# Reordering the opening of an attention kernel: key loads, pooled sums and value sums moved between queues, engines and units

## The chip, the cores and the metric

The kernel runs on one core of one Trainium2 chip. The metric is the device time of one execution in microseconds, taken as the median of several executions. The core has a matrix engine (TensorE, PE in the profile), a vector engine (VectorE, DVE), a scalar engine (ScalarE, ACT), a general engine (GpSimd, POOL) and an engine that mostly starts transfers (SyncE, SP). ACT and POOL start transfers too; each of the three has a queue of its own.

## The reference, cut to what matters

The program computes an attention layer and then two mixture-of-experts layers on its output. The change touches the attention alone:

```python
B, H, S, D = 4, 8, 576, 64          # batches, heads, positions, head size
q_d, k_d, v_d = means over groups of 4 positions of q, k, v     # 144 rows each
out_up   = repeat(softmax(q_d @ k_d.T * scale) @ v_d, 4)        # pooled attention
out_local = softmax(q @ k.T * scale where |i - j| < 4) @ v      # local attention
x = out_up + out_local              # 2304 tokens of 512, input of the experts
```

## The kernel before, in words

The attention is a list of 38 units, numbered here from 0 in the order in which they are pushed. Eighteen are local units, one for each tile of 128 tokens (`Local(t)`); twenty are pooled units, five for each batch (`Pooled(b, u)`). The order is written out by hand: local tiles 0 to 3 are units 0 to 3; batch 0's pooled units are 4, 5, 6, 8 and 9, with tile 4 as unit 7; tile 5 is unit 10, batch 1's pooled units begin at 11, tile 6 is unit 14.

`push(unit)` writes one unit's scores and soft step, the transposes (`turn`) of the unit two before it, the work that was scheduled for this unit (`later`, filled by `schedule(n, f)`, which puts f n units ahead), and the values step (`values`) of the unit three before it. PE, ACT, DVE and POOL carry out their instructions in just this written order. SP's order is set by a planner that sorts transfers by the time at which it believes them ready.

The pooled units need sums over four positions. `pool_qk(b, n)` makes those of queries (`qd`) and keys (`kd`): for batch 0 all on DVE, one reduction for each of twelve 128x576 pieces (the second halves of the keys, `kd[:, i, 1]`, at L776); for batch 1 all on GpSimd, where `pooled_on_gpsimd` makes one 128x576x4 piece in three adds (L759, L789). `pool_v(b, n)` makes the sums of the values (`vd`) on PE with a matrix of ones (`fours`, L798 and L805), which ACT copies out (L800, L809); when it has read batch b's values it starts the load of those of batch b+1, since there is one buffer (`NVG = 1`).

Loads: `load_qk(b)` brings a batch's queries (for batch 1 on GpSimd's queue, else on SP's) and its keys in two halves (SP and ACT). `load_local(t)` brings the value windows of a tile, a half each on SP and ACT. `load_wall` brings the routing weights on GpSimd's queue, copied by DVE `WALLP` units later. Batch 1's key buffer is zeroed by GpSimd first (`zero_keys`), because half of each block must stay zero. `start_1`, `start_2` and `start_3` are done with units 0, 1 and 2: zeroed buffers, distances and masks for the local units, constants for the routing.

Of the kernel before, what the change touches and what calls it, by code (L numbers as in the profile page):

```python
# [15 lines left out]
OP = mybir.AluOpType  # L16
AX = mybir.AxisListType
# [60 lines left out]
D2 = 3  # L78
NEP = 3
EPS = 48  # L80
ONDVE = (0,)
ONPOOLQ, ONPOOLQD, QDP, WALLP = (1,), (2,), 0, 12
NVG = 1
XB = 8
UB = 4
LOADQK = (-1, -1, 5, 9)
POOLQK = (2, 4, 6, 10)
POOLV = (3, 4, 6, 10)
QKS = 4
VS = 0  # L90
PATTERN = ((4, 0, 1), (2, 3))
POOLED = (3, 5, 9, 12)

# [10 lines left out]
def moe_attention_kernel(ctx, tc, q, k, v, w_skip, w_gate, w1, w2, g2, n2, noise, u1, u2, out, dbg=None):  # L104
# [507 lines left out]
    with ExitStack() as actx:  # L612
# [20 lines left out]
        def load_v(b, e=nc.sync):  # L633
            t = ld.tile([128, 4, DM], F32, name="v0", bufs=NVG)
            u = ld.tile([64, DM], F32, name="v1", bufs=NVG)
            r0 = b * S * DM
            e.dma_start(t, v[r0:r0 + 512 * DM].rearrange("(p c d) -> p c d", p=128, d=DM))
            e.dma_start(u, v[r0 + 512 * DM:r0 + S * DM].rearrange("(p d) -> p d", d=DM))
            return t, u
# [12 lines left out]
        def zero_keys(i, e):  # L652
            t = shared.tile([128, 2, 4, S], F32, name=f"kT{i}", bufs=1, tag=f"shared{i}")
            kTs.append(t)
            fill(e, t[:, 0])
            fill(e, t[:, 1])
# [16 lines left out]
        def zero_pooled_exps(e):  # L673

            t = at.tile([128, 2, NPOOL + 16], F32, name=f"ep{len(eps)}", bufs=1)
            e.memset(t[:, :, NPOOL:], 0.0)
            e.memset(t[:, :, NPOOL:NPOOL + 1], 1.0)
            eps.append(t)

        def pooled_ones(e):  # L680


            t = at.tile([128, 2, H, D + 1], F32, name=f"vd{len(vds)}", bufs=1)
            h = H // 2
            e.memset(t[:, 1], 0.0)
            e.memset(t[0:32, 1, :, D:D + 1], 4e-9)
            e.memset(t[0:16, 1, h:, D:D + 1], 0.0)
            e.memset(t[:, 0, :, D:D + 1], 4.0)
            e.memset(t[0:16, 1, 0:h, D:D + 1], 4.0)
            e.memset(t[32:48, 1, h:, D:D + 1], 4.0)  # L690
            vds.append(t)
# [24 lines left out]
        def start_1():  # L716
            for n in range(3, NES):
                zero_exps(P)
            for n in range(3, NVW):
                zero_values(P)  # L720
            zero_keys(1, P)
            pooled_ones(P)
            zero_pooled_exps(P)
            zero_pooled_exps(P)
            for d in offsets:
                distances(d)

        def start_2():
            for n in range(2, NEP):
                zero_pooled_exps(P)  # L730
            pooled_ones(P)
            nc.gpsimd.dma_start(x_d[0:1], kTs[1][0:1, 1, 0, 0:DM + 16])
            for n in range(1, NVG):
                vgs[n] = load_v(n)
            for t in range(2, NVW):
                load_local(t)
            load_qk(1)

        def start_3():
            routing_constants()  # L740
            for d in offsets:
                mask(d)


        fours = at.tile([128, 32], F32, name="fours", bufs=1)
# [2 lines left out]
        def load_qk(b):  # L748

            held["k", b % 2] = b  # L750
            qT[b] = at.tile([128, 4, S], F32, name="qT", bufs=2)
            (nc.gpsimd if b == 1 else nc.sync).dma_start(qT[b], q[b])
            for g in range(2):
                (nc.sync, nc.scalar)[g].dma_start(kTs[b % 2][g:128:2, g], k[b, 64 * g:64 * g + 64])

        def pooled_on_gpsimd(o, x):
            x = x.rearrange("p a (g r) -> p a g r", r=4)
            for j in range(1, 4):
                nc.gpsimd.tensor_tensor(o, x[:, :, :, 0] if j == 1 else o, x[:, :, :, j], op=OP.add)  # L759
# [5 lines left out]
        def pool_qk(b, n):  # L765


            assert held["k", b % 2] == b
            held["kd", b % 2] = (b, n)
            if n == 0 and b not in ONPOOLQD:  # L770
                qd[b] = at.tile([128, 4, NPOOL], F32, name="qd", bufs=2)
            kd, kT = kds[b % 2], kTs[b % 2]
            if n >= 8 and b in ONDVE:
                for i in range(n - 8, 4, 3):
                    o, x = kd[:, i, 1], kT[:, 1, i]
                    nc.vector.tensor_reduce(o, x.rearrange("p (g r) -> p g r", r=4), axis=AX.X, op=OP.add)  # L776
            elif b in ONPOOLQ and n < 8:
                if n == 0:
                    pooled_on_gpsimd(kd[:, :, 0], kT[:, 0])
                    pooled_on_gpsimd(qd[b], qT[b])  # L780
            elif n % 2 == 0 and n < 8 and b in ONPOOLQD:
                pass
            elif n < 8:
                i = n // 2
                o, x = (qd[b][:, i], qT[b][:, i]) if n % 2 == 0 else (kd[:, i, 0], kT[:, 0, i])
                nc.vector.tensor_reduce(o, x.rearrange("p (g r) -> p g r", r=4), axis=AX.X, op=OP.add)
            else:
                o, x = kd[:, :, 1], kT[:, 1].rearrange("p a (g r) -> p a g r", r=4)
                nc.gpsimd.tensor_tensor(o, x[:, :, :, 0] if n == 8 else o, x[:, :, :, n - 7], op=OP.add)  # L789
# [95 lines left out]
        def load_local(t):  # L885

            vw = vws[t % NVW]
            for g in range(2):
                o = N * DM + (2 * t + g) * WV * 1024
                (nc.sync, nc.scalar)[g].dma_start(vw[g:2 * WV:2, g],  # L890
                                  v[o:o + WV * 1024].rearrange("(p s c) -> p s c", s=4, c=256))
# [153 lines left out]
        def schedule(n, f, *args):  # L1045
            later.setdefault(len(pipe) + n, []).append(lambda: f(*args))
# [142 lines left out]
        for t in range(NT):  # L1189
            for b in range(B):  # L1190
                if LOADQK[b] == t:
                    load_qk(b)
                    if b in ONPOOLQD:
                        schedule(QDP, pool_q, b)
                if POOLQK[b] == t:
                    for n in range(8):
                        schedule(n // QKS, pool_qk, b, n)
                    for n in range(3):
                        schedule(n // 2 if b in ONDVE else n, pool_qk, b, n + 8)
                if b == 0 and t == EXP4 and UPE:  # L1200
                    schedule(0, expansion)
                if POOLV[b] == t:
                    schedule(0, pool_v, b, 0)
                    schedule(VS, pool_v, b, 1)
            if t == 3:
                load_wall()
            if t < 3:
                schedule(0, lambda: None)
                schedule(0, lambda: None)
                schedule(0, (start_1, start_2, start_3)[t])  # L1210
            push(Local(t))
            for b, u in pooled_after.get(t, []):
                push(Pooled(b, u))
# [757 lines left out]
```

## Time and profile before

| what | us |
|---|---|
| median of 3 runs (lowest, highest) | 777.15 (775.94, 778.45) |
| the profiled execution | 780.45 |
| its span, first to last instruction | 778.5 |
| outside of the span | 1.95 |
| PE busy in the span | 755.6 (97%) |

The trace is of the one profiled execution, whose time is 3.30 us above the median; differences worked out in it are taken off the median. Times in the rows count from the start of the span. A busy PE counts modelled ends of pipelined matmuls.

### The profile page before, as it was taken

What the parts mean: (1) busy time and instruction counts of PE and PEld (TensorE: products, weight loads), DVE (VectorE), ACT (ScalarE), POOL (GpSimd) and SP (SyncE); (2) the same over time, 40 slices, a digit from 0 to 9 for tenths busy, and PEclk for the clock granted to TensorE, in tenths of its full rate; (3) what the DMA queues carried; (4) which work ended last, traced back from release to release, by engine and by line L of the source; (5) the groups of instructions that cost most, each with busy time, mean ns of one, the idle gap of its engine ahead of it and who ended that gap; (6) DMA issues with size and microseconds to landing.
All of it is one profiled execution on the core that took longest, in us unless ns stands there. A gap on an engine that the chain in (4) does not pass through costs nothing.

```text
span 778.5 us, 15158 instructions
## 1 busy us (share of the span) xinstructions
PE 755.6 (97%) x6215; PEld 664.3 (85%) x6215; DVE 351.3 (45%) x805; ACT 249.6 (32%) x492; POOL 255.0 (33%) x257
## 2 busy tenths in 40 slices
PE   6999998999999999999999999999999999999996
PEld 3567785999999999989998998998998997997984
DVE  8776877510111755469854343262242343342200
ACT  3444553111112133224334343233233242333211
POOL 8782422211232351133364205215115115002012
PEclk9899999999999999999999999999999999999998
DMA  8988578699988872331556626526436336333013
GB/s 287 301 263 272 156 187 283 183 371 355 314 313 259 307 282 97 103 69 43 144 170 172 180 82 166 112 87 174 105 106 159 80 110 159 87 84 67 8 16 46
DMA packets 61128, 131.51 MB, mean 169 GB/s; under 512 B 15585, under 2 KB 16928, under 8 KB 59520
## 3 DMA queue, kind: packets, MB, share of 16 engines
q1 hardware_dynamic: 31552, 56.64, 23.4%
q10 hardware_dynamic: 17248, 46.66, 16.6%
q0 software_dynamic: 12256, 27.21, 16.6%
q8 instruction: 50, 0.82, 0.4%
q14 instruction: 22, 0.18, 0.1%
HBM read 101.86 MB, written 23.91 MB: 162 GB/s over the span
## 4 chain that ended last, share of the span: by engine, by line
PE 76%; issue 2%; DVE 1%; DMA 1%; POOL 0%; ACT 0%; POOLq 0%; DVEq 0%; ACTq 0%
PE pY L1612 27%; PE pH L1595 26%; PE pH L560 9%; PE pY L573 9%; PE pT L1580 2%; PE pT L592 1%; PE pT L539 1%; DMA rows<-x_d,ix2g 1%; PE pT L346 1%; PE pH L581 0%; POOL out L317 0%; DVE w L337 0%; PE pH L597 0%; PE pT L223 0%; DVE hl L1600 0%
## 5 line engine op out<-in xcount | busy, mean ns | idle before, releaser
L1612 PE MATMUL pY<-w,hh 128*128 128x512 f32 (+6 forms) x640 | 201.5, 396 | 0.0
L1595 PE MATMUL pH<-xh,w 128*128 128x256 f32 (+7 forms) x1024 | 196.0, 303 | 0.0
L1595 PEld LDWEIGHTS pH<-xh,w 128*128 128x128 f32 x1024 | 162.9, 188 | 0.8
L1612 PEld LDWEIGHTS pY<-w,hh 128*128 128x128 f32 (+6 forms) x640 | 115.0, 183 | 27.6
L1271 DVE TENSOR_TENSOR w<-stg,w 128x1024 fp32r<-128x1024 f32 x64 | 82.5, 1298 | 108.1 <-ACT w L1270 108.0
L1612 PE MATMUL pY<-w,hl 128*128 128x512 f32 (+6 forms) x320 | 125.6, 393 | 0.0
L1595 PE MATMUL pH<-xl,w 128*128 128x256 f32 (+7 forms) x512 | 123.5, 302 | 0.0
L1600 DVE SCALAR_TENSOR_TENSOR hl<-pH,hh 128x256 fp32r<-128x256 f32 (+7 forms) x128 | 57.0, 474 | 128.8 <-ACT hh L1599 128.5
L317 POOL DMA_INDIRECT out<-yo,ix2w x35 | 68.8, 1967 | 130.0 <-ACT yo L1614 121.5
L1599 ACT ACTIVATE hh<-pH 128x256 fp32r<-128x256 f32 (+7 forms) x128 | 49.3, 424 | 151.8 <-PE pH L1595 151.6
L1595 PEld LDWEIGHTS pH<-xl,w 128*128 128x128 f32 x512 | 90.1, 188 | 0.0
L312 POOL DMA_INDIRECT rows<-x_d,ix2g x32 | 36.2, 1132 | 155.4 <-PE pT L1580 144.2
L1612 PEld LDWEIGHTS pY<-w,hl 128*128 128x128 f32 (+6 forms) x320 | 58.5, 183 | 15.3
L573 PE MATMUL pY<-hT,w 128*128 128x112 f32 (+7 forms) x512 | 69.2, 296 | 0.0
L1270 ACT ACTIVATE w<-stg 128x1024 fp32r<-128x1024 f32 x64 | 66.8, 1054 | 6.8 <-DMA stg<-in_moe_w 6.8
L1614 ACT ACTIVATE yo<-pY,gt 128x512 f32<-128x512 f32 (+6 forms) x35 | 24.1, 688 | 138.3 <-PE pY L1612 77.4
L573 PEld LDWEIGHTS pY<-hT,w 128*128 128x128 f32 x512 | 67.4, 190 | 0.2
L560 PE MATMUL pH<-xT,w 128*128 128x200 f32 (+6 forms) x448 | 66.2, 301 | 0.0
L560 PEld LDWEIGHTS pH<-xT,w 128*128 128x128 f32 x448 | 61.1, 190 | 1.8 <-issue 1.7
L317 POOL DMA_INDIRECT l_d<-x,ix1w x15 | 14.3, 953 | 87.9 <-DVE x L600 87.0
L575 DVE COPY yT<-pY 128x224 f32<-128x224 f32 (+7 forms) x16 | 7.5, 471 | 73.8 <-PE pY L573 73.8
L1006 POOL TENSOR_TENSOR x<-x,up 128x512 f32<-128x512 f32 x15 | 19.3, 1291 | 42.5 <-DMA up<-od 32.6
(426 smaller groups left out, 851.4 us busy)
## 6 DMA issues: line engine op xcount, KB each, us to landing
w<-in_moe_w ACTq DMA_DIRECT2D x16, 2048.0 KB, 12.5
stg<-in_moe_w SPq DMA_DIRECT2D x64, 512.0 KB, 3.6
x_d<-x SPq DMA_DIRECT2D x18, 264.0 KB, 4.1
out<-zero ACTq DMA_DIRECT2D x3, 1536.0 KB, 7.6
up<-od SPq DMA_DIRECT2D x14, 256.0 KB, 5.1
qT<-in_q SPq DMA_DIRECT2D x3, 1152.0 KB, 5.5
vw<-in_v SPq DMA_DIRECT2D x18, 192.0 KB, 5.5
vw<-in_v ACTq DMA_DIRECT2D x18, 192.0 KB, 5.5
```

The source lines that it names most:

```text
L312: return nc.gpsimd.indirect_dma_start(out=dst, out_offset=None, in_=x_d[0:n + 1], in_offset=bass.IndirectOffsetOnAxis(ap=idx, axis=0))
L317: return nc.gpsimd.indirect_dma_start(out=dst, out_offset=bass.IndirectOffsetOnAxis(ap=idx, axis=0), in_=src, in_offset=None, **kw)
L560: nc.tensor.matmul(self.p[:, j], w[:, k, f * 128:(f + 1) * 128], self.xT[:, k], start=k == 0, stop=k == KD - 1)
L573: nc.tensor.matmul(p[:, j], w[:, f, d * 128:(d + 1) * 128], self.hT[:, f], start=f == 0, stop=f == KF - 1)
L1006: e.tensor_tensor(xs[t][:, 0:DM], xs[t][:, 0:DM], ups[t], op=OP.add)
L1270: nc.scalar.activation(hi[:, c], st[i], AF.Copy)
L1271: V.tensor_tensor(lo[:, c], st[i], hi[:, c].bitcast(F32), op=OP.subtract)
L1595: nc.tensor.matmul(p, w[:, k, fs], self.x[ch][n][:, k, 0:ch[1] - ch[0]], start=k == 0 and i == 0, stop=k == KD - 1 and i == 2)
L1599: nc.scalar.activation(hi, p, AF.Relu)
L1600: V.scalar_tensor_tensor(lo, p, 0.0, hi.bitcast(F32), op0=OP.max, op1=OP.subtract)
L1612: nc.tensor.matmul(p, h[:, f], w[:, f], start=f == 0 and i == 0, stop=f == KF - 1 and i == 2)
L1614: nc.scalar.activation(o, p, AF.Copy, scale=gate[0:n])
```

## The change

It alters where and when the attention's opening work is issued; every sum and load is still made once. Batch 0's values are summed with unit 6 (was 3) and batch 1's with unit 11 (was 7), batch 2's with unit 15 (was 14). Batch 0's second-half key sums go from DVE (four reductions) to GpSimd (three adds). Batch 1's queries are loaded on GpSimd's queue right after the key buffer is zeroed, and both halves of its keys on SP's queue. Routing constants (to unit 10), masks (to unit 6), distances and the last zeroed buffers (to unit 3) come later, and so do the routing weights' load (before unit 10) and copy (unit 16).

```diff
-ONDVE = (0,)
-ONPOOLQ, ONPOOLQD, QDP, WALLP = (1,), (2,), 0, 12
+ATONCE = (0,)
+ONPOOLQ, ONPOOLQD, QDP, WALLT, WALLP = (1,), (2,), 0, 5, 6
-POOLV = (3, 4, 6, 10)
+POOLV = (3, 5, 6, 10)
-VS = 0
+VD = (3, 1, 1, 0)
@@ start_1
             zero_keys(1, P)
+            load_qk(1)
             pooled_ones(P)
             zero_pooled_exps(P)
             zero_pooled_exps(P)
+
+        def start_2():
+            for t in range(2, NVW):
+                load_local(t)
+            load_k(1)
+
+        def start_3():
+            schedule(0, start_4)
+            schedule(3, lambda: [mask(d) for d in offsets])
+            schedule(7, routing_constants)
+
+        def start_4():
+            for n in range(2, NEP):
+                zero_pooled_exps(P)
             for d in offsets:
                 distances(d)
-
-        def start_2():
-            for n in range(2, NEP):
-                zero_pooled_exps(P)
             pooled_ones(P)
             nc.gpsimd.dma_start(x_d[0:1], kTs[1][0:1, 1, 0, 0:DM + 16])
-            for n in range(1, NVG):
-                vgs[n] = load_v(n)
-            for t in range(2, NVW):
-                load_local(t)
-            load_qk(1)
-
-        def start_3():
-            routing_constants()
-            for d in offsets:
-                mask(d)
@@ load_qk
             (nc.gpsimd if b == 1 else nc.sync).dma_start(qT[b], q[b])
+            if b != 1:
+                load_k(b)
+
+        def load_k(b):
             for g in range(2):
-                (nc.sync, nc.scalar)[g].dma_start(kTs[b % 2][g:128:2, g], k[b, 64 * g:64 * g + 64])
+                (nc.sync, nc.sync if b == 1 else nc.scalar)[g].dma_start(kTs[b % 2][g:128:2, g], k[b, 64 * g:64 * g + 64])
@@ pool_qk
-            if n >= 8 and b in ONDVE:
-                for i in range(n - 8, 4, 3):
-                    o, x = kd[:, i, 1], kT[:, 1, i]
-                    nc.vector.tensor_reduce(o, x.rearrange("p (g r) -> p g r", r=4), axis=AX.X, op=OP.add)
+            if n >= 8 and b in ATONCE:
+                if n == 8:
+                    pooled_on_gpsimd(kd[:, :, 1], kT[:, 1])
@@ the loop over tiles
-                        schedule(n // 2 if b in ONDVE else n, pool_qk, b, n + 8)
+                        schedule(n // 2 if b in ATONCE else n, pool_qk, b, n + 8)
-                    schedule(0, pool_v, b, 0)
-                    schedule(VS, pool_v, b, 1)
-            if t == 3:
+                    schedule(VD[b], pool_v, b, 0)
+                    schedule(VD[b], pool_v, b, 1)
+            if t == WALLT:
                 load_wall()
```

## Rows read from the trace of the kernel before

**Rows 1.** The page's head and its line of the matrix engine.

```profile
span 778.5 us, 15158 instructions
...
PE 755.6 (97%) x6215; PEld 664.3 (85%) x6215; DVE 351.3 (45%) x805; ACT 249.6 (32%) x492; POOL 255.0 (33%) x257
```

**Rows 2.** Windows: span, busy time (instructions) by engine, PE clock, DMA share.

```profile
core 0: us, PE busy (x) PEld busy (x) DVE busy (x) ACT busy (x) POOL busy (x), PEclk, DMA share, GB/s
0.00:10.00 10.00, 7.90 (x53) 3.22 (x53) 7.03 (x15) 5.30 (x4) 8.79 (x24) 1.00 0.81 289
10.00:20.00 10.00, 5.50 (x124) 3.07 (x117) 9.11 (x20) 1.60 (x4) 8.96 (x37) 0.84 1.01 285
20.00:30.00 10.00, 9.38 (x123) 5.69 (x120) 8.51 (x18) 4.30 (x10) 5.82 (x34) 0.65 1.00 333
...
60.00:70.00 10.00, 10.00 (x164) 7.62 (x156) 6.71 (x20) 5.12 (x16) 1.28 (x1) 1.00 0.84 265
70.00:80.00 10.00, 8.84 (x162) 5.84 (x160) 6.71 (x16) 4.35 (x13) 2.50 (x2) 1.00 0.87 282
```

**Rows 3.** Windows of the two stretches of lower clock.

```profile
16.80:27.00 10.20, 7.59 (x72) 3.62 (x76) 9.30 (x20) 3.70 (x9) 7.24 (x46) 0.50 1.00 342
...
44.10:47.50 3.40, 3.40 (x17) 3.01 (x15) 1.92 (x6) 1.22 (x3) 3.24 (x3) 0.50 0.99 334
```

**Rows 4.** Waits of PE from 14 to 50 us: total, times, longest.

```profile
PE pT L798 <- DMA v<-in_v: 4.7, 2, 4.5
PE pA L832 <- POOL kd L789: 1.8, 1, 1.8
```

**Rows 5.** Timeline of PE: start, length, line, output and input, idle before.

```profile
13.63 0.66 PE L982 MATMUL pT<-ident,e 128*128 128x128 f32 x4
18.79 1.93 PE L798 MATMUL pT<-v,fours 128*32 128x512 f32 x8 [4.50 <-DMA v<-in_v]
...
24.02 1.19 PE L832 MATMUL pA<-kd,qd 128*32 128x288 f32 x8
...
31.73 0.30 PE L951 MATMUL pA<-mask,identb 128*128 128x304 bf16 x1
...
33.35 1.07 PE L798 MATMUL pT<-v,fours 128*32 128x512 f32 x8 [0.18 <-DMA v<-in_v]
34.42 0.61 PE L805 MATMUL pT<-v,fours 64*16 64x256 f32 x4
...
42.97 0.69 PE L832 MATMUL pA<-kd,qd 128*32 128x288 f32 x8 [1.85 <-POOL kd L789]
...
51.19 1.06 PE L798 MATMUL pT<-v,fours 128*32 128x512 f32 x8
```

**Rows 6.** Timeline of POOL, 13 to 43 us.

```profile
13.02 0.52 POOL L685 MEMSET vd<- 128x520 f32 x1
...
14.59 1.65 POOL L702 IOTA dj<- 32x38 f32 x8
...
17.52 0.72 POOL L732 DMA_DIRECT2D x_d<-kT  x1
18.24 0.63 POOL L752 DMA_DIRECT2D qT<-in_q  x1
...
28.38 1.29 POOL L759 TENSOR_TENSOR kd<-kT 128x576 f32<-128x576 f32 x1 [3.94 <-DMA kT<-in_k]
29.74 3.51 POOL L759 TENSOR_TENSOR kd<-kd,kT 128x576 f32<-128x576 f32 x2
...
39.42 3.49 POOL L789 TENSOR_TENSOR kd<-kd,kT 128x576 f32<-128x576 f32 x2
```

**Rows 7.** Timeline of DVE: batch 0's second-half key sums.

```profile
15.99 2.06 DVE L776 TENSOR_REDUCE kd<-kT 128x144 f32<-128x576 f32 x3
```

**Rows 8.** Timeline of ACT's queue: the second half of batch 1's keys.

```profile
18.82 0.52 ACTq L754 DMA_DIRECT2D kT<-in_k  x1
```

**Rows 9.** DMA issues at 18.7, 20, 52.5 and 62.5 us: KB, time to landing.

```profile
kT<-in_k ACTq DMA_DIRECT2D x1, 576.0 KB, 9.4
...
v<-in_v SPq DMA_DIRECT2D x1, 1024.0 KB, 12.4
...
v<-in_v SPq DMA_DIRECT2D x1, 1024.0 KB, 9.2
...
qT<-in_q SPq DMA_DIRECT2D x1, 1152.0 KB, 5.5
```

## The prediction

> **What bounds the kernel now.** I read the page first, then the windows in steps of 10 us, then PE's waits, and then the opening engine by engine. The page says that PE is busy for 97% of the span [rows 1]: the kernel can only get shorter where PE stands still, works at the lower clock, or does work that it need not do. The windows show where that is: PE works 5.50 of the 10 us from 10 to 20, at a mean clock of 0.84, and from 20 to 30 its clock is 0.65 [rows 2]. From 60 to 70 it works without a hole [rows 2], so a unit that starts earlier there ends earlier. PE's waits from 14 to 50 us are nearly two events [rows 4]: 4.5 us for batch 0's values at 18.79, and 1.85 us for a key sum of GpSimd at 42.97 [rows 5]. A low clock follows each: PE runs at the lower of its two levels (0.50, that is 1.2 of 2.4 GHz) from 16.8 to 27.0 and from 44.1 to 47.5 [rows 3], and eight equal matmuls take 1.93 us at 18.79, but 1.07 at 33.35 [rows 5].
>
> The second wait closes a chain that starts in the DMA queues. The second half of batch 1's keys is issued on ACT's queue at 18.82 [rows 8] and lands 9.4 us later [rows 9], at 28.2. GpSimd, idle for 3.94 us by then, starts batch 1's sums at 28.38 and ends them at 39.42 + 3.49 = 42.91 [rows 6]; unit 11's scores start at 42.97 [rows 5]. That chain, 28.4 + 14.5 + 0.1, sets the time of unit 11, and all later PE work hangs on it. What the change is worth is read there.
>
> **Part 1: batch 0's key sums and value sums.** Before, PE reads the values' sums in front of unit 0's values step and waits for them. With the sums at unit 6, it goes on after its transposes at 13.63 + 0.66 = 14.3 [rows 5] with unit 0's values (its window must have landed, as ACT's copy must; both were asked for by then), and then meets unit 4's scores, which need the batch's key sums. On GpSimd these now stand behind the key buffer's zeroing (ends at 13.0), the issue of batch 1's queries (0.63 and a gap, 0.7) and 1.57 us of small fills (13.02 to 14.59); the three adds cost what the same three cost for batch 1, 28.38 to 29.74 + 3.46, that is 4.82 us [rows 6]. Sum: 13.0 + 0.7 + 1.6 + 4.8 = 20.1. DVE's eight other reductions are shorter than that once four of 0.66 to 0.74 us (three in 2.06 [rows 7]) are gone. So unit 4's scores start at 20.1, where they stood at 24.02 [rows 5].
>
> The row says that four reductions of DVE (2.7 us) become 4.8 us of GpSimd. The Trainium skill, GPSIMD Engine Reference, section Engine selection, speaks against that: it puts reductions along the free dimension on VectorE and calls GpSimd about half as fast for adds of two inputs. Left on DVE, by that rule, the sums would come behind DVE's other reductions, some 2.7 us after about 19.7, so 22.4; the engine's lower rate would then matter only if GpSimd were the later one. No run here shows it yet.
>
> **Part 2: batch 1's loads.** The queries' issue moves from 18.24 [rows 6] to 13.1, the keys' second half from 18.82 [rows 8] to 13.1, as soon as its buffer is zeroed; both halves now queue on SP behind the first windows, and ACT is not held by that issue. How early do they land? Not earlier than 13.1 + 9.4 = 22.5, not later than the 28.2 of before. Asked for by 13.7 are queries and keys of two batches, one batch of values and four windows, by their sizes 7.47 MB in all; the first 20 us move 2.89 + 2.85, and the rest of 1.73 MB takes 5.2 us at 333 GB/s [rows 2], so everything has landed by 25.2. The keys stand in front of the queries in this line, so I take 24.3. GpSimd is then free: after the adds at 20.1 it has distances (1.7), fills (1.2) and the zero row's transfer (0.7) to do, spans 14.59 to 18.24 of before [rows 6], which ends at 23.75. Batch 1's sums take 14.5, as before: unit 11 may start at 24.3 + 14.5 + 0.1 = 38.9, instead of 42.97.
>
> Does PE get there by then? From unit 4 to unit 7 it took 31.73 - 24.02 = 7.7 us, from there to its wait 41.1 - 31.7 = 9.4 [rows 5]. It gains batch 0's value sums (1.07 + 0.61 = 1.7) and loses batch 1's (1.7, and 0.2 of waiting). If the low clock lasts to 27.0 as before, 3.9 us more of this work lies in it than before and cost 2 us more: 20.1 + 7.7 + 1.7 + 2.0 = 31.5, then 9.4 - 1.9, so 39.0. If the higher level is back a third sooner, 37.2. I take 39.0 for unit 11: both chains meet there. That is 4.0 us earlier than before.
>
> **Part 3: what then follows unit 11.** Batch 1's value sums stood in the shadow of that wait; now they come behind it: 1.6 us of PE at the high level [rows 5] that nothing covers. For the low stretch behind unit 11 (3.4 us at half rate, 1.7 us lost [rows 3]) I take the value of before, as PE may still wait up to 1.8 us; the other end is that it is gone. Routing constants (18.9 to 22.2 before, 3.3 us) and the weights' transfers (2.2 us) stood in front of GpSimd's wait for the keys, and now stand behind batch 1's sums: GpSimd gets to its first residual add some 0.9 us later than the 52.65 of before, while PE needs it at about 57.7 - 2.4; this stays covered, and if it were not it would cost what is missing of the 1.7 us left. Masks, distances and wall copy lie beside other work on DVE, cover for about 2 us of them being PE's own queue.
>
> Sum: -4.0 + 1.6 = -2.4 us on a profiled 780.45, so 778.05 for an execution like that one, and 777.15 - 2.4 = **774.7** as the median, as that execution lies 3.3 us above it.
>
> **Rivals.**
> *No low stretch behind unit 11.* If PE arrives no earlier than the sums, as the sum above has it, PE never rests before 11 and the 1.7 us stay: 774.7 - 1.7 = 773.0. For it speaks that the only two low stretches of the opening follow holes of PE [rows 3, 5]; against it, that PE's arrival has 2 us of uncertainty.
>
> *The keys land no earlier.* The engines are at shares of 1.01 and 1.00 from 10 to 30 us [rows 2]; an earlier issue then only divides the same bandwidth. Unit 11 stays at 42.8, the value sums are added: -0.2 + 1.6 = 778.5. Against it: 1.73 MB remain at 20 us, not more. The Trainium skill, DMA: Bandwidth & Descriptors, section Issuing engines are not separate DMA queues, says just this of moving a transfer to another engine's queue: it saves the issue time alone. By that rule the move from ACT to SP gives nothing, and only the earlier time of issue can; the shares in the trace agree with a full set of engines.
>
> *The third batch's values come late* (the other side). Their one buffer is free only when batch 1's sums have read it, now behind unit 11: 39.0 + 1.0 for scores and transposes + 1.0, issue at 41.0, 42.0 in a low stretch, instead of 34.5. PE asks for them at unit 15, in the place of 51.19 [rows 5]: 51.19 - 2.4 + 1.2 for the pooled unit now in front = 50.0. The load has 8 us. Loads of this kind took 9.2 and 12.4 us with other megabytes in the queue, a load of 1152 KB with little in front took 5.5 [rows 9]; since batch 2's queries and keys have by then had the queue for themselves, I take 7.5, no stall. At 12.4 PE waits 4.4 and falls to the low level once more: 774.7 + 4.4 + 1.7 = 780.8. It is slower than the bound from 11.1 us of landing on.
>
> *Given back later.* From 60 to 80 us the DMA share is 0.84 and 0.87, and PE has a hole of 1.2 us from 70 to 80 [rows 2]. If loads there set the pace, units 11 to 20 come earlier and wait there: 777.1.
>
> **How the numbers follow.** A difference of 0.3% (2.3 us; 774.8 and 779.5) is about what a measurement of this kernel can tell from none. Chances: forecast 0.36 (its own range 773.6 to 775.8, a little over half of it under 774.8); no low stretch 0.20, faster; keys no earlier 0.16, same but for 0.04 slower; third values late 0.16, of this 0.13 slower; given back 0.12, same. Faster 0.20 + 0.20 = 0.40, same 0.16 + 0.12 + 0.03 + 0.12 = 0.43, slower 0.04 + 0.13 = 0.17. The time is 774.7; the range reaches from 772.3, under the second case with keys at 23.8, to 779.5, which leaves out most of the late values.
>
> **What will show it.** Right: no wait for values before unit 0's values step; unit 4's scores at about 20; batch 1's sums on GpSimd from 24 to 39; unit 11 at 39 with value sums right behind it; from there to 120 us the same rows, some 2.4 us earlier. Wrong: keys landing at 27 or later, GpSimd not free when they land, PE waiting for batch 2's values at unit 15, or SP holding a transfer behind the two key halves so that windows come late.

## The result: 0.64% slower, and the profile after

Over twelve executions each the changed kernel takes 785.49 us (782.42 to 788.68) and the one before 780.62 us (775.94 to 784.0): ratio 1.0064, interval 1.0042 to 1.0086. Forecast was 774.7, with 779.5 as the upper end. Of the 10.8 us between forecast and time 3.5 lie in the base: 777.15 was the median of three executions of the kernel before, 780.62 is that of twelve. The profiled execution of after took 785.6 us, its span 783.6, which is 5.1 us longer than that of before [rows 1].

The page's head and its line of PE, after:

```profile
span 783.6 us, 15153 instructions
...
PE 756.6 (97%) x6212; PEld 667.1 (85%) x6215; DVE 356.6 (46%) x801; ACT 251.0 (32%) x492; POOL 257.8 (33%) x260
```

PE is busy 1.0 us longer than before, in that longer span: the rest is PE standing still. The timeline of PE after (columns as in [rows 5]; lines are 4 higher than before: scores are L833 and L836, value sums L802 and L809):

```profile
20.26 1.24 PE L836 MATMUL pA<-kd,qd 128*32 128x288 f32 x6 [1.95 <-POOL ep L676]
22.15 0.67 PE L836 MATMUL pA<-kd,qd 128*32 128x288 f32 x2 [0.65 <-DVE kd L790]
...
27.49 1.07 PE L802 MATMUL pT<-v,fours 128*32 128x512 f32 x8
...
30.94 0.29 PE L955 MATMUL pA<-mask,identb 128*128 128x304 bf16 x1 [0.83 <-DVE mask L710]
...
36.10 1.30 PE L870 MATMUL pB<-vd,epT 128*128 128x130 f32 x6 [2.14 <-DVE x L1004]
...
42.31 0.67 PE L836 MATMUL pA<-kd,qd 128*32 128x288 f32 x8
...
43.39 1.06 PE L802 MATMUL pT<-v,fours 128*32 128x512 f32 x8
...
80.25 0.71 PE L1016 MATMUL pT<-ident,x 128*128 128x128 f32 x4 [2.85 <-POOL x L1010]
```

Unit 4 starts at 20.26, unit 7 at 30.94, near the forecast (20.1 and 31.5); the releaser printed at 20.26, `POOL ep`, is the small fill that follows GpSimd's key sums, which end at 20.21. Unit 7 is there by another sum than the forecast's, though: 2.0 us had been counted for a low clock up to 27.0, and in this profile the clock is 1.00 from 13 to 36; the waits of 0.65 us for VectorE's key sums and 0.83 for a mask stand in its place. From unit 7 to unit 11 PE takes 11.4 us where 7.5 were forecast, and unit 11 is at 42.31, not 39.0. GpSimd is not the reason here; its timeline (idle before in brackets) shows batch 0's second-half sums, batch 1's, and the residual add of tile 4:

```profile
15.34 1.28 POOL L764 TENSOR_TENSOR kd<-kT 128x576 f32<-128x576 f32 x1
16.70 3.51 POOL L764 TENSOR_TENSOR kd<-kd,kT 128x576 f32<-128x576 f32 x2
...
24.67 1.25 POOL L764 TENSOR_TENSOR kd<-kT 128x576 f32<-128x576 f32 x1 [1.01 <-DMA kT<-in_k]
...
29.46 1.25 POOL L764 TENSOR_TENSOR qd<-qT 128x576 f32<-128x576 f32 x1
30.79 3.49 POOL L764 TENSOR_TENSOR qd<-qd,qT 128x576 f32<-128x576 f32 x2
...
35.59 3.45 POOL L793 TENSOR_TENSOR kd<-kd,kT 128x576 f32<-128x576 f32 x2
...
78.94 1.26 POOL L1010 TENSOR_TENSOR x<-x,up 128x512 f32<-128x512 f32 x1 [14.94 <-DMA up<-od]
```

The keys' first sum starts at 24.67 and the sums are done at 39.04: both as forecast (24.3, 38.9). What PE waits for is VectorE, whose timeline has the four mask operations, now at unit 6; the first fence is after, the second the first two of the same four before:

```profile
29.08 0.48 DVE L709 TENSOR_TENSOR mscr<-dj 128x38 f32<-128x38 f32 x1
29.59 1.29 DVE L710 TENSOR_SCALAR mask<-mscr 128x304 bf16<-128x304 f32 x1
30.99 1.56 DVE L709 TENSOR_TENSOR mscr<-dj 128x38 f32<-128x38 f32 x1
32.59 1.87 DVE L710 TENSOR_SCALAR mask<-mscr 128x304 bf16<-128x304 f32 x1
```

```profile
17.97 0.19 DVE L709 TENSOR_TENSOR mscr<-dj 128x38 f32<-128x38 f32 x1
18.19 0.32 DVE L710 TENSOR_SCALAR mask<-mscr 128x304 bf16<-128x304 f32 x1
```

They take 5.2 us in all instead of 1.0, beside GpSimd's adds, and what stands behind them (the output x of a local unit) comes late. The second loss is at tile 4's turn, 80.25, behind a residual add for which GpSimd waits 14.94 us. SyncE's queue, after and then before, tells why: the four pieces of the pooled part read from the routed rows (`up<-or`) went out at 55.48, and now stand behind three stores of the residual (`x_d<-x`), with the piece `up<-od` behind them:

```profile
64.06 3.21 SPq L1043 DMA_DIRECT2D x_d<-x  x2
...
70.28 0.32 SPq L1043 DMA_DIRECT2D x_d<-x  x1
71.78 3.23 SPq L916 DMA_DIRECT2D up<-or  x4
75.10 0.54 SPq L912 DMA_DIRECT2D up<-od  x1
```

```profile
55.48 3.00 SPq L912 DMA_DIRECT2D up<-or  x4
...
64.58 3.14 SPq L1039 DMA_DIRECT2D x_d<-x  x2
67.81 0.58 SPq L908 DMA_DIRECT2D up<-od  x1
```

Windows of after (columns as in [rows 2]), the three stretches of lower clock up to 150 us:

```profile
36.30:39.80 3.50, 3.50 (x16) 3.11 (x16) 2.91 (x10) 1.75 (x4) 3.42 (x4) 0.51 0.83 348
80.70:84.10 3.40, 3.40 (x18) 2.67 (x20) 3.37 (x8) 0.93 (x2) 3.13 (x3) 0.50 0.87 204
135.30:142.20 6.90, 6.73 (x41) 6.61 (x42) 3.75 (x18) 0.90 (x2) 0.00 (x0) 0.51 1.00 323
```

The first two follow the two waits above. The third stands at the end of the attention, where the profile of before had none. It begins with the first transposes of the gathered rows, after and then before:

```profile
135.20 0.93 PE L539 MATMUL pT<-ident,xr 112*128 112x112 f32 x4 [1.47 <-DMA xr<-x_d,ix0g]
```

```profile
132.84 0.60 PE L539 MATMUL pT<-ident,xr 112*128 112x112 f32 x4 [0.75 <-DMA xr<-x_d,ix0g]
```

So of the 5.1 us between the two spans 2.4 have come up by this point, and 2.7 behind it, where the change touches nothing.

### The profile page after: what moved, and what is told of

Same layout as the page of the kernel before. It is cut to its first block, busy times and chain, and to the rows that moved or that the text cites. A ratio compares the mean times of both kernels' runs of the same rounds, so it can differ in the third digit from the quotient of the medians.

```text
span 783.6 us, 15153 instructions
## 1 busy us (share of the span) xinstructions
PE 756.6 (97%) x6212; PEld 667.1 (85%) x6215; DVE 356.6 (46%) x801; ACT 251.0 (32%) x492; POOL 257.8 (33%) x260
## 4 chain that ended last, share of the span: by engine, by line
PE 77%; issue 1%; DVE 1%; DMA 1%; POOL 0%; ACT 0%; POOLq 0%; DVEq 0%; ACTq 0%
PE pY L1616 27%; PE pH L1599 27%; PE pH L560 9%; PE pY L573 9%; PE pT L1584 2%; PE pT L592 1%; PE pT L346 1%; PE pT L539 1%; DMA rows<-x_d,ix2g 1%; PE pH L581 0%; POOL out L317 0%; DVE w L337 0%; PE pH L597 0%; PE pT L223 0%; DVE hl L1604 0%
```

## The experiments

Three theories of the loss came out of the two traces. A: the masks beside GpSimd's adds. B: SyncE's order at tile 4. C: the low stretch at the end. Ratios are to the kernel before on the same chip, with 95% intervals, twelve executions of each unless said. The kernels of a table were timed together on one chip (in the third table the first four, and apart from them the last two); from one table to another, and to the 1.0064 of the change, only the ratios can be compared, and two of them that lie 0.002 to 0.003 apart have intervals that overlap.

### The three theories, one by one and together

**Masks early** (diff on after):

```diff
-            schedule(3, lambda: [mask(d) for d in offsets])
+            schedule(0, lambda: [mask(d) for d in offsets])
```

Expected: 

> The changed kernel, but the two masks are made with unit 3 instead of unit 6, before GpSimd starts batch 1's sums. Theory A (the four mask instructions of VectorE stand behind GpSimd's adds there): they take about 1.1 us again instead of 5.3, the waits of TensorE of 0.83 and 2.14 us at units 7 and 9 and the stretch of lower clock from 36.3 go, unit 11 starts 3 to 4 us earlier, at about 39; the time against the kernel before falls from 1.0064 to 1.001 to 1.003. Theory B (what costs is the place of tile 4's pooled rows in SyncE's queue): unit 11 may move, but TensorE waits for tile 4's residual add as long as its rows land at 78, ratio 1.005 to 1.0065. Theory C (the stretch of lower clock at 135 to 142 us makes the loss): ratio unchanged unless that stretch goes.

**Routed pieces on GpSimd's queue** (on after; tile 4 alone):

```diff
-                        nc.sync.dma_start(up[o, i * 128:(i + 1) * 128],
+                        (nc.gpsimd if t == 4 else nc.sync).dma_start(up[o, i * 128:(i + 1) * 128],
```

Expected: 

> The changed kernel, but the four small copies that bring tile 4's pooled rows of batch 0 are issued on GpSimd's queue instead of SyncE's. Theory B (in SyncE's order they and the fifth now stand behind three stores, so that the residual add of tile 4 starts at 78.9 instead of 75.4): the wait of TensorE of 2.85 us before tile 4's transposes and the stretch of lower clock from 80.7 go, the part up to 120 us is 2.5 to 4 us shorter, ratio 1.001 to 1.003. Theory A (masks): ratio stays at 1.005 to 1.0065. Theory C: the same.

**Filler at the end** (on after; eight matmuls without use instead of three while PE waits for the gathered rows):

```diff
-"part16": 1, "end": 3}
+"part16": 1, "end": 8}
```

Expected: 

> The changed kernel with eight instead of three filler matmuls at the attention's end, where TensorE waits 1.5 us for the gathered rows before it turns them. Theory C (that rest is what the lower clock from 135 to 142 us follows, which costs 3.4 us): no lower clock there, ratio 1.001 to 1.003. Theories A and B: the lower clock there is one execution's chance or follows an earlier rest; ratio stays at 1.005 to 1.007.

**All three edits.** Expected: 

> The changed kernel with masks at unit 3, tile 4's rows of batch 0 on GpSimd's queue and eight filler matmuls at the end. If A, B and C add up: 4 + 3 + 3 us less than the changed kernel, ratio 0.993 to 0.997, as was forecast for the change itself or better. If only one of them carries the loss: that one's ratio, 1.001 to 1.003. If the loss is none of these: 1.005 or more.

| kernel | ratio | interval |
|---|---|---|
| masks early | 1.0071 | 1.0046 to 1.0095 |
| routed pieces on GpSimd's queue | 1.0039 | 1.0021 to 1.0057 |
| filler at the end | 1.0065 | 1.0044 to 1.0085 |
| all three | 1.0046 | 1.0021 to 1.0071 |

Only B moves the time: the two kernels with its edit are on average 2.0 us, 0.26%, faster than the two without (24 executions each; 95% interval 0.8 to 3.3 us, worked out from the single times). The filler gains nothing with B's edit or without it. PE at tile 4's turn, with the routed pieces on GpSimd's queue:

```profile
77.93 0.63 PE L1016 MATMUL pT<-ident,x 128*128 128x128 f32 x4 [0.25 <-ACT vd L804]
```

The wait of 2.85 us is gone. This is the fastest of that kernel's twelve executions (780.25 us, median 782.48), but the other traces say the same: PE waits 1.41 to 3.12 us for tile 4's residual add in the five where the routed pieces stand behind stores, and in one only (1.26 us) of the eight of the change with the pieces on GpSimd's queue, those of later experiments included. With the masks early they take 0.19 to 0.32 us each, so theory A is right about the operations; but in that trace another wait stands at unit 11, and the ratio does not fall, so it is wrong about the time:

```profile
26.97 1.32 POOL L764 TENSOR_TENSOR kd<-kT 128x576 f32<-128x576 f32 x1 [3.00 <-DMA kT<-in_k]
...
41.51 0.69 PE L836 MATMUL pA<-kd,qd 128*32 128x288 f32 x8 [2.54 <-POOL kd L793]
```

GpSimd had the keys at 26.97 in this execution, not at 24.67. In the filler's trace the end has no low stretch, yet its ratio is that of after.

### One part of the change alone

On the kernel before, each with its lines of the diff shown ahead: the value sums' new places alone (`POOLV`, `VD`); batch 1's loads alone (`load_qk(1)` in `start_1`, `load_k(1)` in `start_2`, both halves on SyncE's queue); batch 0's second-half key sums on GpSimd alone (`ATONCE`). And after with the value sums of batches 1 and 2 back at units 7 and 14:

```diff
-POOLV = (3, 5, 6, 10)
-VD = (3, 1, 1, 0)
+POOLV = (3, 4, 6, 10)
+VD = (3, 0, 0, 0)
```

Values alone, expected: 

> The kernel before with the positions of the value sums alone (all three batches), nothing else of the change. In the order written for SyncE, tile 4's four pieces of the pooled part that come out of the routed rows then stand behind the third residual store, as in the changed kernel. Theory B (that order costs 2 to 3 us): unit 4 starts near 21, earlier than 24.0, unit 11 stays near 43, since batch 1's keys are as before; tile 4's turn waits about 3 us as in the changed kernel, with a low stretch from about 80.7, and the ratio to before is 1.003 to 1.007. Rival (the order is harmless, the loss sits in the opening, in masks and key sums): the hole in front of unit 0's values is gone and nothing comes in its place, ratio 0.996 to 1.000.

Loads alone, expected: 

> The kernel before with batch 1's loads alone: queries asked for right after the key buffer is zeroed, both halves of the keys on SyncE's queue. SyncE's order at tile 4 is that of before. Theory: the keys land at 24.5 to 27 instead of 28.2, batch 1's sums end at 39.5 to 41.5, PE's wait at unit 11 (1.85 us) goes or shrinks, unit 11 at 41 to 42; tile 4's turn has no wait over 0.5 us; ratio 0.996 to 1.000. Rival (the earlier transfers take the bandwidth of batch 0's values and windows): the wait for batch 0's values grows beyond 4.5 us and unit 4 starts after 24.5; ratio 1.001 to 1.004.

Key sums alone, expected: 

> The kernel before with batch 0's second-half key sums on GpSimd instead of VectorE, nothing else. Before, PE reached unit 4 behind its wait for values, so if that wait is what counts, unit 4 stays at 24.0 and the ratio is 0.999 to 1.001. Rival (GpSimd's adds hold VectorE up, as they did the masks in the changed kernel, and delay GpSimd's own constants): operations of VectorE beside the three adds are two to five times as long as before, unit 4 or a local unit waits for VectorE, GpSimd reaches the keys of batch 1 late; unit 11 at 44 to 45, ratio 1.001 to 1.003.

After with later values back, expected: 

> The changed kernel with batch 1's and batch 2's value sums back at their old places (units 7 and 14), batch 0's at unit 6 as changed. SyncE's order then has three of tile 4's four routed pieces ahead of the stores. Theory B together with an uncovered sum behind unit 11: the wait at tile 4's turn shrinks from 2.85 to under 1.5 us, unit 14 comes about 1.6 us earlier after unit 11, and the ratio to before falls from 1.006 to 0.997 to 1.002. Rival (the remaining loss of 2 to 3 us sits elsewhere: masks, low stretches, later key landings): it stays at 1.003 to 1.005, as with the routed pieces on GpSimd's queue.

| kernel | ratio | interval |
|---|---|---|
| values alone (6 executions) | 1.0118 | 1.0079 to 1.0157 |
| loads alone | 0.9989 | 0.9964 to 1.0014 |
| key sums alone | 1.0022 | 0.9997 to 1.0047 |
| after, batches 1 and 2 back | 1.0060 | 1.0030 to 1.0090 |

No part is a measurable gain. The values alone are worse than the whole change; PE's timeline there:

```profile
24.20 1.17 PE L832 MATMUL pA<-kd,qd 128*32 128x288 f32 x4 [4.76 <-DVE kd L776]
...
54.35 1.07 PE L798 MATMUL pT<-v,fours 128*32 128x512 f32 x8 [2.50 <-DMA v<-in_v]
...
82.10 0.66 PE L1012 MATMUL pT<-ident,x 128*128 128x128 f32 x4 [2.53 <-POOL x L1006]
```

Without the wait for values PE comes to unit 4 early and waits there for VectorE's key sums; the one value buffer is read later, so batch 2's values come late; and tile 4 waits as in after. The last one (after with batches 1 and 2 back) missed both expectations on time: at unit 7 PE waits 2.52 us for batch 1's values, since their load still starts only when batch 0's sums, at unit 6, have read the buffer.

### With the order of tile 4 mended

All have tile 4's routed pieces on GpSimd's queue, as above: the kernel before as a control; after with all value sums at their old places; after with batch 0's sums at unit 4 and the others at their old places; after with batch 0's second-half key sums on VectorE. The last three on after, beside the edit of the routed pieces:

```diff
-POOLV = (3, 5, 6, 10)
-VD = (3, 1, 1, 0)
+POOLV = (3, 4, 6, 10)
+VD = (0, 0, 0, 0)
...
+POOLV = (3, 4, 6, 10)
+VD = (1, 0, 0, 0)
...
-                if n == 8:
-                    pooled_on_gpsimd(kd[:, :, 1], kT[:, 1])
+                for i in range(n - 8, 4, 3):
+                    o, x = kd[:, i, 1], kT[:, 1, i]
+                    nc.vector.tensor_reduce(o, x.rearrange("p (g r) -> p g r", r=4), axis=AX.X, op=OP.add)
```

Control, expected: 

> A control: the kernel before with tile 4's four routed pieces on GpSimd's queue, as in the second experiment, and nothing of the change. Before has no wait over 0.9 us at tile 4's turn, so there is nothing to win there: if the four issues cost GpSimd nothing that counts, the ratio is 0.998 to 1.001, and the gain of the second experiment (2.5 us) is the gain of the mended order. Rival (GpSimd's issues cost something themselves, so that the order is worth more than 2.5 us): ratio 1.002 or more.

Values at the old places, expected: 

> The changed kernel with all three value sums at their old places (units 3, 7 and 14) and tile 4's routed pieces on GpSimd's queue: of the change the earlier loads, the key sums on GpSimd and the later masks and constants are left. Theory V (what is left of the loss after the order is mended, 2.9 us, comes from the value sums' places: the hole moves from the values to the key sums, the one value buffer is read later and its next load lands late): ratio 0.997 to 1.000. Theory K (it comes from the key sums on GpSimd and from what they push back on GpSimd and VectorE): ratio 1.002 to 1.005; unit 4 at 23 to 24, unit 11 at 42 to 44.

Batch 0's values at unit 4, expected: 

> The changed kernel with batch 0's value sums with unit 4 (behind its scores, which wait for the key sums till 20.2 in any case), batch 1's and 2's at units 7 and 14, and tile 4's routed pieces on GpSimd's queue. The values have landed by then (18.8), the load of batch 1's values is asked for at 23 to 24 instead of 28.6, so batch 1's sums need not wait at unit 7. Theory V: ratio 0.995 to 0.999, unit 4 at 20.3, unit 11 at 40.5 to 42, no wait for values over 0.7 us. Theory K: 1.002 to 1.005, as in the second experiment.

Key sums on VectorE, expected: 

> The changed kernel with batch 0's second-half key sums back on VectorE and tile 4's routed pieces on GpSimd's queue. Theory K: the loss of 2.9 us of the second experiment goes, ratio 0.999 to 1.001. Theory V: VectorE's eight other reductions come first, as in the trace with the values alone, where the last parts of unit 4 started at 24.20 after a wait of 4.76 us for them; so unit 4 is late, the ratio 1.004 to 1.010, and the move of the key sums was a gain for the kernel with the other parts of the change.

Then the third of these with the masks at unit 3 as well (`schedule(0, ...)`, as in the first experiment), and that kernel with the sums of batches 1 and 2 at units 11 and 15 again (`POOLV = (3, 5, 6, 10)`, `VD = (1, 1, 1, 0)`):

Masks early too, expected: 

> The kernel of the eleventh experiment (the changed one with batch 0's value sums at unit 4, batch 1's and 2's at units 7 and 14, tile 4's routed pieces on GpSimd's queue) with the masks made at unit 3, before GpSimd's adds for batch 1 begin. Theory M (the masks beside GpSimd's adds hold PE up, and with batch 1's value sums in front of unit 11 that counts): masks at 0.2 to 0.3 us each, no wait for a mask, unit 7 at 29.5 to 30.5, unit 11 at 40.5 to 42 held by GpSimd's sums, unit 14 at 46 to 47.5, ratio 0.996 to 0.999. Rival (the masks are hidden anyway by GpSimd's chain to unit 11, which ends at 40 to 41.5 with or without them): 1.000 to 1.002, as in the eleventh experiment.

Later values behind unit 11, expected: 

> The kernel of the thirteenth experiment with batch 1's value sums behind unit 11 and batch 2's with unit 15, as in the change. By the prediction's third part these sums cost 1.6 us there, since PE waits in front of unit 11 in either case; batch 2's values are then asked for at 44 instead of 33 and may be late. So the ratio is 0.002 to 0.004 above that of the thirteenth. Rival (PE arrives at unit 11 no earlier than GpSimd's sums end, so nothing is uncovered): within 0.001 of the thirteenth.

| kernel | ratio | interval |
|---|---|---|
| before, routed pieces moved | 0.9987 | 0.9961 to 1.0013 |
| after, values at old places | 1.0033 | 1.0006 to 1.0060 |
| after, batch 0's values at unit 4 | 1.0019 | 0.9995 to 1.0044 |
| after, key sums on VectorE | 1.0058 | 1.0034 to 1.0082 |
| batch 0's values at unit 4, masks early | 1.0014 | 0.9989 to 1.0039 |
| the same, later values behind unit 11 | 1.0036 | 1.0012 to 1.0061 |

The control says that moving the pieces costs nothing that can be measured; its interval, from 0.9961, does not exclude a small gain by the move itself. The theory that the key sums on GpSimd are the loss falls: with them back on VectorE the ratio is 1.0058, where that theory asked for 0.999 to 1.001. The values at their old places decided little: that trace has 1.45 and 2.12 us of wait for values again and, at unit 7, 1.78 for a mask. The last pair bears on the third part's term: with the value sums behind unit 11 the ratio is 0.22% higher, 1.7 us, where the forecast had 1.6. That is not clear of noise: the means of the two kernels lie 1.1 us apart, with an interval of -1.0 to 3.2.

### The two kernels again, and the loads back

Three more profiled executions, one timing each: before twice, after once. Then the kernel with batch 0's values at unit 4 and masks early, with batch 1's loads as before:

```diff
-            load_qk(1)                  # start_1
...
-            load_k(1)                   # start_2
+            load_qk(1)                  # start_2
...
-            if b != 1:                  # load_qk
-                load_k(b)
+            load_k(b)
...
-(nc.sync, nc.sync if b == 1 else nc.scalar)[g]
+(nc.sync, nc.scalar)[g]
```

Before again, expected: 

> The kernel before, unchanged, one more profiled execution. If the late keys are typical of it, GpSimd's first sum of batch 1's keys starts at 28 or later after an idle time of over 3 us, and unit 11 at 42.5 or later with PE waiting 1.5 us or more. If they were that one execution's, it starts at 24.5 to 27 and unit 11 at 40.5 to 42.5 with a wait under 1 us.

After again, expected: 

> The changed kernel, unchanged, one more profiled execution. By the twelve traces with these loads GpSimd's first sum of batch 1's keys starts at 25.5 to 27.4, that is one to three us later than in the first profile of it (24.67), PE waits 2 to 4 us in front of unit 4, unit 11 is at 40.5 to 43, and tile 4's turn waits about 3 us.

Before a third time, expected: 

> The kernel before, unchanged, a third profiled execution; the same two cases as for the second: 28 or later if the late keys are typical of it, 24.5 to 27 if not.

Loads back, expected: 

> The kernel of the thirteenth experiment with batch 1's loads as before: queries and first key half with unit 1, the second half of the keys on ACT's queue. If the loads of the change bring the keys later, GpSimd's first sum of these keys starts at 23.5 to 25 (26.88 in the thirteenth), its sums end at 38 to 39.5 instead of 41.3, unit 11 is at 39 to 40, and the ratio is 0.995 to 0.999, under that of the thirteenth by 0.002 or more: a version faster than both kernels. Rival (the landing is set by the bytes asked for in all, not by their order): first sum at 26 to 27.5, ratio 1.000 to 1.002.

The second and the third profile of before, GpSimd's first and last sum of batch 1's keys and PE's unit 11:

```profile
24.60 1.36 POOL L759 TENSOR_TENSOR kd<-kT 128x576 f32<-128x576 f32 x1
...
36.41 3.50 POOL L789 TENSOR_TENSOR kd<-kd,kT 128x576 f32<-128x576 f32 x2
...
41.47 0.47 PE L832 MATMUL pA<-kd,qd 128*32 128x288 f32 x2
```

```profile
24.63 1.23 POOL L759 TENSOR_TENSOR kd<-kT 128x576 f32<-128x576 f32 x1
...
37.07 3.49 POOL L789 TENSOR_TENSOR kd<-kd,kT 128x576 f32<-128x576 f32 x2
...
43.72 0.67 PE L832 MATMUL pA<-kd,qd 128*32 128x288 f32 x8
```

No idle time stands before the first sums: the keys had landed by then. GpSimd is done at 39.91 and 40.56, and PE does not wait for it at unit 11. (In the second profile PE stands still for 1.25 us shortly before unit 11, for nothing that the profile shows; without that it would be there at 40.2, still behind the sums.) The control, whose opening is that of before, says the same: first sum at 24.46, sums done at 40.06, unit 11 at 41.99 without a wait. The 3.94 us of idle time at 28.38 and PE's 1.85 us behind it [rows 5, 6] were that one execution's. Before took 778.96 and 781.72 us in the two new executions, after 783.75.

| trace | first key sum of batch 1 (idle before) | sums end | unit 4 | unit 11 | unit 14 |
|---|---|---|---|---|---|
| before [rows 5, 6] | 28.38 (3.94) | 42.91 | 24.02 | 42.97 | 49.81 |
| before, second | 24.60 (0) | 39.91 | 22.27 | 41.47 | 46.83 |
| before, third | 24.63 (0) | 40.56 | 20.60, its last part 25.91 | 43.72 | 48.89 |
| after | 24.67 (1.01) | 39.04 | 20.26, its last part 22.15 | 42.31 | 49.21 |
| after, second | 25.47 (1.76) | 39.93 | 20.30 | 41.72 | 48.61 |

The second profile of after waited for a mask (0.71 us), for an x of VectorE (2.16) and at tile 4 (1.41). The loads back gave 1.0019, interval 1.0001 to 1.0037, with the keys no earlier:

```profile
27.30 1.32 POOL L762 TENSOR_TENSOR kd<-kT 128x576 f32<-128x576 f32 x1 [3.54 <-DMA kT<-in_k]
```

So its expectation of a version faster than both kernels did not come true, and no kernel here is measurably faster than before.

## Why the prediction was wrong, step by step

**What bounds the kernel: the step that failed first.** "That chain, 28.4 + 14.5 + 0.1, sets the time of unit 11, and all later PE work hangs on it." It did so in one execution. In two further ones PE gets to unit 11 at 41.47 and 43.72 and GpSimd is done before. The 4.0 us to be won there were a property of the trace that was read, not of the kernel. With the control, that makes three executions of four with the opening of before in which the chain did not hold unit 11. By unit 14, in front of which both kernels have summed batch 1's values, before stands at 48.5 as the mean of its three traces and after at 48.9 of its two; with the control (47.15) on the one side, and the traces with the routed pieces moved and with the filler (49.48 and 47.85, the opening of after) on the other, at 48.2 and 48.8. So no gain of the opening is to be seen, where the forecast put it 2.4 us ahead.

**Part 1, key sums and value sums: right in GpSimd's sum.** Unit 4 at 20.26, 20.1 forecast. But the wait is moved, not removed: PE waits 1.95 to 4.37 us there for GpSimd's key sums, in the place of the values. And VectorE's eight other reductions, which the forecast had done by then, are not always: in the first profile they end at 22.09, and the last two of unit 4's eight matmuls start at 22.15; VectorE is the later of the two in four of the eleven traces where PE meets unit 4 this way. On the choice of engine: with the sums on VectorE unit 4's last part starts at 24.36, where the prediction worked out 22.4; in that trace these reductions start 2.0 us later than in before (17.99 for 15.99), behind an early operation of VectorE that took 3.60 us where most traces have 1.64. The ratio is 1.0058 there and 1.0039 with the sums on GpSimd; the intervals overlap, so the time does not decide between the engines. The rule of the Trainium skill that the prediction cites, GPSIMD Engine Reference, section Engine selection, would put them on VectorE; no gain by that shows here.

**Part 2, the keys: right in the first profile by luck.** 24.3 forecast, 24.67 there; but in the thirteen other traces with batch 1's queries asked for at about 13 (14.6 in one), the first sum of the keys starts at 25.47 to 27.38 after 1.76 us of idle time or more. Of the five traces of before, and of before with one edit, that keep the old loads and let GpSimd get there early enough to tell, it starts at 24.46, 24.60 and 24.63 without idle time, at 25.35 after 0.92, and at 28.38 in the profile that was read. In the two later profiles of before GpSimd waits for the queries instead (0.68 and 1.46 us), and its sums end at the same time as after's, 39.9 to 40.6 against 39.0 to 39.9. So in these traces the change trades late queries for late keys. That is the rival "the keys land no earlier". The Trainium skill, DMA: Bandwidth & Descriptors, section Issuing engines are not separate DMA queues, says the same of a move between queues, and these traces agree. That the earlier queries take the bandwidth from the keys fits all of them but was not isolated by a run: in the run with the loads back the queries still went out at 14.6, and the keys' second half at 13.4, where before has 18.2 and 16.9 to 18.8.

**"Masks, distances and wall copy lie beside other work on DVE": the second step that failed.** Beside GpSimd's adds the masks took 5.2 us and not 1.0, and PE's own queue did not cover it. The Trainium skill, SBUF — State Buffer, section Who interferes with whom, says that VectorE and GpSimd share a pair of memory ports, held by one instruction while the other blocks, for operations of VectorE that read two inputs from that memory or use a two-port mode. The rows agree: in after each long mask operation ends within 0.2 us of the end of one of GpSimd's adds (30.88 against 30.71, 34.46 against 34.28, and 32.55 against 32.54, the middle of the pair at 30.79). In time nothing of it can be told: with the masks early the ratio moves by +0.0007 in one pair and -0.0005 in the other. In the first of these traces PE then waits 2.54 us at unit 11 for GpSimd's sums instead; in the second unit 11 is 1.7 us earlier than without the edit (41.42 for 43.13), and why the time does not show it stays open.

**Part 3: not contradicted, 1.7 us for 1.6 in a pair that noise alone could give.** The value sums do stand uncovered behind unit 11 in the traces, 1.6 us of them at the high level. That batch 2's values might then be late (the rival of the other side) was seen too, but seldom: 1.69 us of wait in one trace and 2.50 in another of twenty.

**What the forecast didn't have: SyncE's order at tile 4.** It held that from unit 11 "to 120 us the same rows" would follow. But the planner sorts SyncE's transfers by its own times, and later value sums alone turn its order at 55 to 75 us. No rival had it; "given back later" looked at the right stretch for another reason. It costs 2.0 us (0.8 to 3.3) by the four kernels of the first table; the control (0.9987, 0.9961 to 1.0013) shows no gain of the edit alone that is clear of noise, but would not exclude one of this size.

**The sum.** Forecast -2.4; measured +0.64%, about 5.0 us. The -4.0 of unit 11 is the term that failed: the chain that it rests on held unit 11 in one execution of four, and in the two profiles of after unit 11 is at 42.31 and 41.72 where before has 41.47 to 43.72. Shown in time is the order of SyncE's queue, 2.0 us. The value sums behind unit 11 add 1.7 us by the forecast's own account, which the one pair fits without proving it. Without the -4.0 and with 2.0 for the queue the forecast's own sum is +3.6 us, inside the measured interval (3.3 to 6.7). With the order mended, the later value sums back, batch 0's at unit 4 and the masks early, 1.0014 is left, which can't be told from nothing; the later routing constants, routing weights and zeroed buffers are still in that kernel, and no run has put them back alone.

The traces cut the loss another way. Up to the first transposes of the gathered rows the profiles of after are 2.0 us later than those of before (135.20 and 132.23; 132.84, 129.95 and 132.37). The rest of the span, where the change touches nothing, takes 648.4 and 649.7 us against 645.7, 647.3 and 647.5: 2.2 us more. Both profiles of after have a low stretch there, 6.9 and 6.8 us long; of the three of before one has 3.4 us near there, from 127.1. With filler the stretch was gone in the trace and the rest took 646.0 us, yet the ratio stayed. So how the earlier slips lead to the stretch, and whether it is a part of the 5 us or of these executions, stays open.

## What to carry to other kernels

A wait in one trace is not yet a wait of the kernel: where a forecast hangs on when a transfer lands in a crowded queue, look at two or three profiled executions first. When a wait is taken away, name what PE meets next and when that is ready; here the holes at 18.8 and 43 came back as holes at 20, at 31 to 36 and at 80. And where a planner orders a queue, a change in one place is a change of the whole order: compare the written order of every queue before trusting that the rest stays.

## What the runs showed of the hardware

The same transfer can take some 4 us more or less from one execution to the next: the second half of batch 1's keys, 576 KB, landed 9.4 us after its issue at 18.82 in the first profile of before [rows 8, 9], and 5.5 us after its issue at 17.63 in the control, whose opening is the same. In the later profiles of before it was issued at 17.76 and 16.86 and had landed by 24.6, so within 6.9 and 7.8 us.

Short operations of VectorE grow up to eightfold beside GpSimd's adds (in after 0.32 to 1.29 and 1.87 us, 0.19 to 1.56), while reductions of matmul results beside the same adds keep their length (0.45 to 0.47 us at 28.23, 35.87 and 37.16 in after, 0.45 to 0.47 in before). An early operation with GpSimd's fills beside it took 1.64 us in thirteen of the twenty traces, 3.60 in five and 5.55 in two, the first profile of after among them, where PE waited 2.10 us for what stood behind it. Each time it ended within 0.1 us of the end of one of the fills (in after these end at 9.08, about 11.0 and 12.99):

```profile
7.51 5.55 DVE L1176 TENSOR_SCALAR before<-jp 128x128 bf16<-128x128 f32 x1
```
